# Beacon attention with a maxout FFN on one core: batch 0's waits, an order of scores, and the order of three loads

## The chip, the core and the metric

The kernel runs on one core of one Trainium2 chip. The core has a matrix engine (PE, whose weight loads are listed apart as PEld), a vector engine (DVE), a scalar engine (ACT), a general engine (POOL), and SP, which here only starts DMA transfers. Each engine takes its own instructions strictly in the order in which the program wrote them, and waits for others by semaphores. DMA transfers are started from SP's, ACT's and POOL's streams. The metric is the time of one execution on the device in microseconds (us); a kernel's time is the median of several.

## What is computed

```python
def _attn_ref(q, k, v, beacon_k, beacon_v):       # B=8, H=8, S=576, Nb=16, D=64
    k_all = np.concatenate([beacon_k, k], axis=2)
    v_all = np.concatenate([beacon_v, v], axis=2)
    scores = scale * np.matmul(q, k_all.transpose(0, 1, 3, 2))
    causal = np.zeros((S, Nb + S), dtype=bool)
    causal[:, Nb:] = np.triu(np.ones((S, S), dtype=bool), k=1)
    scores = np.where(causal, -1000000000.0, scores)
    a = np.exp(scores - scores.max(-1, keepdims=True))
    a /= a.sum(-1, keepdims=True) + 1e-09
    return np.matmul(a, v_all)

def _moe_ref(x, w1, w2, w3, w_out):               # 4608 tokens, 512 -> 768 -> 512
    h = np.maximum(np.maximum(x @ w1, x @ w2), x @ w3)
    return h @ w_out
```

The attention's output, with its heads side by side, is x. Inputs and output are float32; the kernel computes in bfloat16 with float32 sums.

## The kernel before

**Tiles.** Two heads make a pair `p` (four pairs in a batch), two pairs a quad (two quads in a batch), so batch 0 holds pairs 0 to 3 and quads 0 and 1, and quad 2 is the first of batch 1. Queries and keys of a pair are needed with the head dimension on the partitions, so PE transposes ("turns") them into PSUM, and DVE or ACT copies the result into `qkT`. The scores of a pair are made in four groups `(p, 0)` to `(p, 3)`: PE writes a group into one of two `sc` buffers (L464), ACT takes its exponential into `at_sb` (L473), and DVE (L490) or POOL (L492) zeroes what the causal mask removes. Then PE multiplies with the values and with ones (the row sums) for a quad and a half of its queries: `P(quad, half, apart, first, last)` is that step or some of its four passes (L536). ACT inverts the sums by Ln and Exp (`invert_sums`, L556 and L558), DVE multiplies (`multiply`, L568) into `xT`, the FFN's input. `F(n)` makes n units of the FFN; the first ones in batch 0 are half-units of eight 256-column matmuls (L615) into `fps`. The first three of these use weight 0, the next three weight 1.

**Order.** The order is written out by hand: `start()`, then the list `first_steps` for batch 0, whose entries each give a group of scores to be made and the functions to be called after it, then a planned loop for the other batches. In the list:

- `T(p, h, pv, q_copy, idle)` turns half h of pair p (`turn_half`, L393): six transposes of queries into one PSUM bank, six of keys into another, each followed by a copy into `qkT` (L413). `pv` says whether the banks are the two `pv` banks or two buffers of `fps`, which has two. `idle` transposes of a constant tile `busy` may be put ahead (`fill`, L387), into a part of the bank that nobody reads.
- `keep_busy(n, cols, ffn)` (L429) makes n matmuls of `busy`, 128 x `cols`, that nobody reads, into the bank `pv1` or a buffer of `fps`.
- `M(p, g, dve)` is the mask of a group, on DVE or POOL. `V(t)` is POOL's cast of a part of batch 0's values, `cast_p` POOL's cast of beacon keys.
- `load_w(i, 0, d_ff)` (L309) is two requests on POOL for weight i, with a cast to bfloat16 on the way.
- `G(0)` is `load_wide` (L182) for quad 2's queries, with a gate: DVE sets one column of the staging tile to zero (L187), and the request on SP waits for that. `load_wide(n_quad, 1)` is the same for the keys, with no gate. `CW(2, i)` is POOL's cast of these (L237), `turn_quad` and `TW` are PE's turns of them (L373) and their copies (L380).
- `next_load(n)` takes the next n loads from a list: SP's requests for quad 3 and batch 1's values, further on quad 4 and so on.

SP's stream holds only requests and their waits, so those of `next_load` follow the gated request of quad 2 as soon as they stand next, whatever the other engines do. A staging tile `st` is one of eight; the casts free it.

Of the kernel before, what the change touches and what calls it, by code (L numbers as in the profile page):

```python
# [16 lines left out]
def kernel(  # L17
# [19 lines left out]
    d_model, d_ff = moe_w1.shape  # L37
# [26 lines left out]
    n_quad = 2  # L64
# [99 lines left out]
    def pv_bank(i, shape, dtype):  # L164
        return pv_psum.tile(shape, dtype, name=f"pv{i}")
# [221 lines left out]
    def fill(ps, n):  # L387

        for i in range(n):
            x0 = 512 + 128 * (i % 4)  # L390
            nc.tensor.transpose(ps[:, x0 : x0 + 128], busy[:, 0:128], ident)

    def turn_half(p, h, pv, q_copy=None, idle=0):  # L393
        for i in range(2):
            src = stage.pop(("half16", p, h, i))
            if pv:
                bank = pv_bank(i, [128, 1024], BF16)
            else:
                bank = ffn_psum.tile([128, 1024], BF16, name="fps")
            ps = bank[:, 0:HALF]  # L400
            if i == 0:
                fill(bank, idle)
            for r in range(HR):
                for e in range(2):
                    nc.tensor.transpose(  # L405
                        ps[64 * e : 64 * e + 64, r * QP : (r + 1) * QP],
                        src[:, e, r],
                        ident[0:QP, 0:QP],
                        tile_position=(0, 64 * e),
                    )  # L410
            x0 = i * Nb + HALF * h
            dst = (qTs, kTs)[i][p % NT][:, x0 : x0 + HALF]
            (q_copy if i == 0 and q_copy else by_dve)(  # L413
                dst.rearrange("d (p r) -> d p r", r=HR), ps.rearrange("d (r p) -> d p r", r=HR)
            )
# [272 lines left out]
    def emit_ffn(limit, pool=None, name="fps"):  # L688
        if done[0] == len(units):
            return False  # L690
        need, fn, args = units[done[0]]
        if done[0] + 1 <= limit + 1e-6 and need <= ready[0]:
            fn(*args, pool or ffn_psum, name)
            done[0] += 1
            return True
        return False
# [8 lines left out]
    def L(fn, *a):  # L705
        return lambda: fn(*a)
# [28 lines left out]
    def start():  # L735
# [22 lines left out]
        cast_half(0, 1, by_act)  # L758
        by_dve(bk16_0, bk32_0)
        turn_half(0, 0, False, by_act)  # L760
        keep_busy(4)
        turn_beacons(0, 1, bk16_0)
        by_act(qk_all[:, 1:PPB, S : S + Nb], bT[:, 1:PPB, 0:Nb])
        cast_half(1, 0, by_dve)
        cast_half(1, 1, by_dve)
        keep_busy(2)
        turn_half(1, 0, True, by_act)

    pv_at = {}
# [4 lines left out]
    def steps(p):  # L774
        return [[0, 1], [2, 3]]

    def T(p, h, pv, q_copy=None, idle=0):
        def run():
            turn_half(p, h, pv, q_copy, idle)

        return run

    def M(p, gi, dve=False):
        return L(emit_masks, p, gi, dve)

    def P(quad, hf, apart=False, first=0, last=len(passes)):
        return L(emit_pv, quad, hf, first, last, apart)

    def V(t):
        return L(cast_first_v, t)  # L790

    def G(i):
        return L(load_wide, n_quad, i, nc.vector)

    def F(n):
        return lambda: [emit_ffn(END) for _ in range(n)]

    def CW(quad, i):
        return L(cast_wide, quad, i, by_pool)

    def TW(quad, i, n, act=False):
        return L(turn_wide, quad, i, n, by_act if act else by_dve, False)

    def cast_p():
        for g in range(n_quad):
# [6 lines left out]

    first_steps = [
        ((0, 0), [T(2, 0, False)]),
        ((1, 0), [T(3, 0, True, None, 4), L(next_load, 2), V(0)]),
        ((2, 0), []),
        ((3, 0), [T(0, 1, False, None, 4), M(0, 0, True), V(1), L(load_w, 0, 0, d_ff), V(2)]),
        ((0, 1), [T(1, 1, True), M(1, 0, True), M(0, 1)]),
        ((0, 2), [T(2, 1, False), M(2, 0, True), M(0, 2), V(3), V(4), L(load_w, 1, 0, d_ff)]),
        ((0, 3), [T(3, 1, False), M(3, 0, True), M(0, 3, True)]),  # L820
        ((1, 1), [M(1, 1)]),
        ((1, 2), [P(0, 0, False, 0, 2), M(1, 2)]),
        ((1, 3), [P(0, 0, False, 2, 4), invert_sums, M(1, 3, True)]),
        ((2, 1), [P(1, 0, True, 0, 2), multiply, M(2, 1), cast_p]),
        ((2, 2), [P(1, 0, True, 2, 4), invert_sums, M(2, 2, True), G(0), L(load_wide, n_quad, 1)]),
        ((2, 3), [P(0, 1, False, 0, 2), multiply, M(2, 3), CW(2, 0), L(load_w, 2, 0, d_ff)]),
        ((3, 1), [P(0, 1, False, 2, 4), invert_sums, F(1), M(3, 1, True)]),
        ((3, 2), [F(1), multiply, L(turn_beacons, 1, B_PE, bk16_1), L(next_load, 5), M(3, 2, True)]),
        ((3, 3), [F(1), M(3, 3, True), CW(2, 1), L(turn_quad, 2, 0), F(1), TW(2, 1, 0), P(1, 1), invert_sums, TW(2, 1, 1, True),
                  L(place_quad_beacons, 2, by_act), F(1), multiply]),  # L830
    ]
    at_step(4, 0, C(cast_wide, 3, 0, by_pool))
# [7 lines left out]
    for b in range(2, B):  # L840
        p = b * PPB
# [6 lines left out]
    for b in range(B_PE, B):  # L848
        p = b * PPB
# [117 lines left out]
```

The softmax here doesn't subtract the row's maximum and nothing guards it: scores larger than these inputs give would overflow.

## Time and profile before

| | |
|---|---|
| median of 4 runs | 300.56 us (298.3 to 300.96) |
| profiled execution | 300.96 us, its span 299.2 us |
| mean granted PE clock | 0.98 |
| HBM read, written | 35.13 MB, 14.22 MB |
| PE's share of the chain that ended last | 88% |

The span runs from the first to the last recorded instruction; the execution's own time is somewhat longer. In the chain that ended last one follows, from the last instruction back, what released each step. PE's instructions around the change, in order of time, are these (start us, us, engine, line, operation, tiles; in brackets the idle time before it and what ended it):

```profile
9.41 0.40 PE L464 MATMUL sc<-qkT 64*128 64x288 bf16 x6
10.27 0.40 PE L464 MATMUL sc<-qkT 64*128 64x288 bf16 x6 [0.47 <-DVE qkT L413]
10.60 0.40 PE L391 MATMUL fps<-ident,busy 128*128 128x128 bf16 x4
10.93 0.45 PE L405 MATMUL fps<-ident,quad 96*64 96x96 bf16 x12
11.80 0.63 PE L464 MATMUL sc<-qkT 64*128 64x288 bf16 x4 [0.43 <-DVE qkT L413]
12.36 0.45 PE L405 MATMUL pv<-ident,quad 96*64 96x96 bf16 x12
12.73 0.33 PE L464 MATMUL sc<-qkT 64*128 64x288 bf16 x4
13.00 0.32 PE L405 MATMUL fps<-ident,quad 96*64 96x96 bf16 x6
13.55 0.32 PE L405 MATMUL fps<-ident,quad 96*64 96x96 bf16 x6 [0.24 <-DMA quad<-in_k_dram]
13.80 0.30 PE L464 MATMUL sc<-qkT 64*128 64x288 bf16 x2
14.56 0.81 PE L405 MATMUL fps<-ident,quad 96*64 96x96 bf16 x12 [0.46 <-DVE qkT L413]
```

The first line is scores (2, 0), the second (3, 0); then come T(0, 1) with its four fillers, (0, 1), T(1, 1), (0, 2), T(2, 1) in two halves, (0, 3), and T(3, 1), which waits for DVE to copy T(2, 1) out of the two `fps` buffers. A few more rows that the prediction uses: ACT stands idle 1.15 us before the exponential of (1, 1) at 15.94, whose matmuls PE made from 15.30. POOL casts the last values of batch 0 at 17.83 for 1.17 us, requests weight 1 at 18.94, has masks at 20.02 for 1.05 us and `cast_p` at 21.02 for 0.74 us. DVE's mask of (1, 3) is at 18.62 for 0.64 us. Weight 1's two requests took 6.4 and 7.8 us to land.

### The profile page before, as it was taken

The numbers are of one execution on the slowest core, as the hardware profiler recorded it, in microseconds if no ns is written. First come the engines' busy times: TensorE is split into PE (matmuls) and PEld (weight loads), VectorE is DVE, ScalarE is ACT, GpSimd is POOL, SyncE is SP. The second block draws the span as 40 slices with busy tenths as digits, with TensorE's granted clock in tenths as the row PEclk, the third lists the DMA queues.
The fourth block names the chain that finished last, engine by engine and source line by source line (L and its number), as shares of the span: only waits on it lengthen the run. The fifth ranks groups of instructions, "written<-read, shape, count | busy, mean of one in ns | idle before, by whom it ended". The sixth has DMA issues, their size and how long they took to land.

```text
span 299.2 us, 8565 instructions
## 1 busy us (share of the span) xinstructions
PE 286.4 (96%) x3548; PEld 152.9 (51%) x3548; DVE 173.4 (58%) x341; ACT 147.1 (49%) x231; POOL 121.6 (41%) x241
## 2 busy tenths in 40 slices
PE   8798899999999999999999999999999999999992
PEld 4545676454545445444546777544454554444441
DVE  3765565546666665646664656466646665373571
ACT  3875488856665355545555555455546521302200
POOL 7361398455456454637363736373415100000000
PEclk9958999999999999999999999999999999999998
DMA  8999979989938999999979999899431003003003
GB/s 157 206 170 319 231 210 296 196 276 251 211 84 199 205 242 221 196 198 255 235 183 223 238 253 203 187 186 234 110 128 37 2 2 123 18 3 140 0 10 133
DMA packets 83590, 50.66 MB, mean 169 GB/s; under 512 B 64224, under 2 KB 75232, under 8 KB 83552
## 3 DMA queue, kind: packets, MB, share of 16 engines
q1 hardware_dynamic: 77904, 45.50, 65.7%
q0 software_dynamic: 4048, 4.03, 8.4%
q10 hardware_dynamic: 1600, 0.59, 0.9%
q8 instruction: 28, 0.46, 0.7%
q14 instruction: 10, 0.08, 0.1%
HBM read 35.13 MB, written 14.22 MB: 165 GB/s over the span
## 4 chain that ended last, share of the span: by engine, by line
PE 88%; DVE 4%; ACT 3%; POOL 1%; DMA 1%; issue 1%; DVEq 0%
PE fps L596 32%; PE pv L536 13%; PE sc L596 12%; PE fps L632 10%; PE sc L464 10%; PE sc L632 4%; PE fps L615 2%; PE pv L432 2%; ACT at_sb L473 1%; PE pv L373 1%; DMA out_dram<-y 1%; DVE xT L568 1%; DVE qkT L380 1%; POOL p L237 1%; PE fps L405 1%
## 5 line engine op out<-in xcount | busy, mean ns | idle before, releaser
L473 ACT ACTIVATE at_sb<-sc 128x928 bf16<-128x928 f32 (+5 forms) x128 | 103.8, 861 | 86.5 <-PE sc L464 84.6
L596 PE MATMUL fps<-xT,w_sb 128*128 128x512 bf16 (+1 forms) x488 | 110.2, 357 | 0.5 <-DVE xT L568 0.5
L492 POOL TENSOR_SCALAR_AFFINE_SELECT at_sb<-at_sb 128x256 bf16<-128x256 bf16 (+2 forms) x146 | 53.4, 386 | 103.8 <-ACT at_sb L473 102.8
L596 PEld LDWEIGHTS <-w_sb 128*128 128x128 bf16 x672 | 61.6, 98 | 65.0 <-issue 12.0
L606 DVE TENSOR_TENSOR hT<-hT,fps 128x512 bf16<-128x512 bf16 x72 | 49.4, 688 | 33.8 <-PE fps L596 33.8
L596 PE MATMUL sc<-xT,w_sb 128*128 128x512 bf16 (+1 forms) x184 | 42.1, 356 | 0.0
L464 PE MATMUL sc<-qkT 64*128 64x288 bf16 (+5 forms) x400 | 36.7, 284 | 2.3 <-DVE qkT L413 0.9
L632 PE MATMUL fps<-w_out_sb,hT 128*128 128x512 bf16 x150 | 36.0, 379 | 0.0
L640 DVE COPY y<-fps 128x512 f32<-128x512 f32 x25 | 17.3, 692 | 27.6 <-PE fps L632 26.3
L632 PEld LDWEIGHTS <-hT 128*128 128x128 bf16 x210 | 19.8, 98 | 24.0 <-DVE hT L606 1.9
L606 DVE TENSOR_TENSOR hT<-hT,sc 128x512 bf16<-128x512 bf16 x30 | 20.6, 688 | 16.4 <-PE sc L596 16.2
L536 PE MATMUL pv<-at_sb,v_sb 128*32 128x288 bf16 (+5 forms) x1376 | 29.7, 232 | 0.0
L604 DVE CAST hT<-fps 128x512 bf16<-128x512 f32 x31 | 21.4, 692 | 12.8 <-PE fps L596 12.8
L568 DVE TENSOR_TENSOR xT<-pv,recip 128x288 bf16<-128x288 f32 (+2 forms) x93 | 27.3, 348 | 2.3 <-ACT recip L558 2.2
L464 PEld LDWEIGHTS <-qkT 64*128 64x128 bf16 x400 | 14.5, 95 | 26.4 <-issue 18.9
L536 PEld LDWEIGHTS <-v_sb 128*32 128x32 bf16 (+1 forms) x1408 | 24.9, 98 | 3.3 <-issue 1.7
L248 POOL CAST p<-st 96x768 bf16<-96x768 f32 x32 | 25.6, 826 | 0.0
L287 POOL CAST v_sb<-st 128x1536 bf16<-128x1536 f32 (+2 forms) x21 | 18.4, 897 | 0.0
L536 PE MATMUL pv<-at_sb,ones 128*32 128x288 bf16 (+4 forms) x500 | 17.7, 263 | 0.0
L556 ACT ACTIVATE lnd<-pv 128x288 f32<-128x288 f32 x31 | 12.9, 416 | 8.0 <-PE pv L536 8.0
L237 POOL CAST p<-st 128x1152 bf16<-128x1152 f32 x12 | 13.7, 1145 | 5.5 <-DVE xT L568 5.5
L604 ACT CAST hT<-sc 128x512 bf16<-128x512 f32 x6 | 3.5, 586 | 23.7 <-PE sc L596 23.7
(73 smaller groups left out, 173.6 us busy)
## 6 DMA issues: line engine op xcount, KB each, us to landing
out_dram<-y SPq DMA_DIRECT2D x35, 256.0 KB, 2.4
st<-in_v_dram SPq DMA_DIRECT2D x23, 256.0 KB, 6.8
st<-in_q_dram SPq DMA_DIRECT2D x16, 288.0 KB, 4.3
st<-in_k_dram SPq DMA_DIRECT2D x16, 288.0 KB, 5.2
st<-in_q_dram SPq DMA_DIRECT2D x6, 576.0 KB, 6.5
st<-in_k_dram SPq DMA_DIRECT2D x6, 576.0 KB, 7.1
w_sb<-in_moe_w_dram POOLq DMA_DIRECT2D x6, 384.0 KB, 7.4
q_dram<-p SPq DMA_DIRECT2D x16, 144.0 KB, 2.3
```

Source lines behind the costliest of these rows:

```text
L248: cast(part.rearrange("p r h d -> p h r d"), st[0:QP, i * NQ2 : (i + 1) * NQ2].rearrange("p (h r d) -> p h r d", h=2, r=QR),)
L287: cast(v_sb[0:n, t:t1].rearrange("p t h d -> p (t h d)"), st[0:n, (t - t_lo) * H * D : (t1 - t_lo) * H * D],)
L464: nc.tensor.matmul(ps[:, e, off : off + q1 - q0], kT[hs, 128 * t : 128 * t + 128], qT[hs, q0:q1], start=True, stop=True, tile_position=(64 ...
L473: nc.scalar.activation(out=both_heads(p, gi), in_=ps[:, :, 0 : g_width(p, gi)], func=AF.Exp, scale=scale)
L492: nc.gpsimd.affine_select(out=view, in_=view, compare_op=ALU.is_ge, fill=0.0, base=x0, pattern=[[0, 2], [1, hi - lo]], channel_multiplier=-1,)
L536: nc.tensor.matmul(ps[bank][32 * j : 32 * j + 32, lo + q0 - qa : lo + qb - qa], lhsT, at_view(pair_of(quad, j)[0], t, pair_of(quad, j)[1], ...
L568: nc.vector.tensor_mul(xT[:, 2 * g + part - 1, c0 + ca : c0 + cb], ps[bank][:, lo : lo + cb - ca], recip[:, ca:cb],)
L596: nc.tensor.matmul(ps[:, o0 : o0 + n], w_in[i][:, ct, 128 * ft : 128 * (ft + 1)], xT[:, ct, x0 : x0 + n], start=(ct == 0), stop=(ct == n_c ...
L604: (by_act if alone[0] else by_dve)(h, ps)
L606: nc.vector.tensor_max(h, h, ps)
L632: nc.tensor.matmul(ps, hT[:, ft, 128 * tt : 128 * (tt + 1)], w_out_sb[:, ft, :], start=(ft == 0), stop=(ft == n_ft - 1),)
L640: nc.vector.tensor_copy(y, ps)
```

## The change

The numbers of `idle` become two, so that the key bank of a turn can have fillers too. `keep_busy` stands at three more places. Scores (1, 1) go ahead of T(3, 1), and T(3, 1)'s mask with it. `G(0)` and the key load go from step (2, 2) to step (1, 3). Weight 1 goes from step (0, 2) to (2, 1), behind `cast_p`; weight 2 from (2, 3) to (3, 3), behind `CW(2, 1)`. In the last step the fourth half-unit of the FFN goes behind the first turn of quad 2's keys.

```diff
-    def turn_half(p, h, pv, q_copy=None, idle=0):
+    def turn_half(p, h, pv, q_copy=None, idle=(0, 0)):
...
-            if i == 0:
-                fill(bank, idle)
+            fill(bank, idle[i])
...
-        ((1, 0), [T(3, 0, True, None, 4), L(next_load, 2), V(0)]),
-        ((2, 0), []),
-        ((3, 0), [T(0, 1, False, None, 4), M(0, 0, True), V(1), L(load_w, 0, 0, d_ff), V(2)]),
+        ((1, 0), [T(3, 0, True, None, (4, 0)), L(next_load, 2), V(0)]),
+        ((2, 0), [L(keep_busy, 2, 320, True)]),
+        ((3, 0), [T(0, 1, False, None, (4, 0)), M(0, 0, True), V(1), L(load_w, 0, 0, d_ff), V(2), L(keep_busy, 2)]),
         ((0, 1), [T(1, 1, True), M(1, 0, True), M(0, 1)]),
-        ((0, 2), [T(2, 1, False), M(2, 0, True), M(0, 2), V(3), V(4), L(load_w, 1, 0, d_ff)]),
-        ((0, 3), [T(3, 1, False), M(3, 0, True), M(0, 3, True)]),
-        ((1, 1), [M(1, 1)]),
+        ((0, 2), [T(2, 1, False, None, (0, 6)), M(2, 0, True), M(0, 2), V(3), V(4)]),
+        ((0, 3), [M(0, 3, True), L(keep_busy, 2)]),
+        ((1, 1), [T(3, 1, False), M(3, 0, True), M(1, 1)]),
         ((1, 2), [P(0, 0, False, 0, 2), M(1, 2)]),
-        ((1, 3), [P(0, 0, False, 2, 4), invert_sums, M(1, 3, True)]),
-        ((2, 1), [P(1, 0, True, 0, 2), multiply, M(2, 1), cast_p]),
-        ((2, 2), [P(1, 0, True, 2, 4), invert_sums, M(2, 2, True), G(0), L(load_wide, n_quad, 1)]),
-        ((2, 3), [P(0, 1, False, 0, 2), multiply, M(2, 3), CW(2, 0), L(load_w, 2, 0, d_ff)]),
+        ((1, 3), [P(0, 0, False, 2, 4), invert_sums, M(1, 3, True), G(0), L(load_wide, n_quad, 1)]),
+        ((2, 1), [P(1, 0, True, 0, 2), multiply, M(2, 1), cast_p, L(load_w, 1, 0, d_ff)]),
+        ((2, 2), [P(1, 0, True, 2, 4), invert_sums, M(2, 2, True)]),
+        ((2, 3), [P(0, 1, False, 0, 2), multiply, M(2, 3), CW(2, 0)]),
         ((3, 1), [P(0, 1, False, 2, 4), invert_sums, F(1), M(3, 1, True)]),
         ((3, 2), [F(1), multiply, L(turn_beacons, 1, B_PE, bk16_1), L(next_load, 5), M(3, 2, True)]),
-        ((3, 3), [F(1), M(3, 3, True), CW(2, 1), L(turn_quad, 2, 0), F(1), TW(2, 1, 0), P(1, 1), invert_sums, TW(2, 1, 1, True),
+        ((3, 3), [F(1), M(3, 3, True), CW(2, 1), L(load_w, 2, 0, d_ff), L(turn_quad, 2, 0), TW(2, 1, 0), F(1), P(1, 1), invert_sums, TW(2, 1, 1, True),
                   L(place_quad_beacons, 2, by_act), F(1), multiply]),
```

More of the change, by code (lines that the diff above doesn't have):

```diff
@@ L775, in steps, with T @@
         return [[0, 1], [2, 3]]
-    def T(p, h, pv, q_copy=None, idle=0):
+    def T(p, h, pv, q_copy=None, idle=(0, 0)):
         def run():
```

## The prediction

> **What bounds the kernel now.** First the head of the page: who is busy, and at which granted clock. (Tenths in 40 slices of 7.48 us.)
>
> ```profile
> span 299.2 us, 8565 instructions
> PE 286.4 (96%) x3548; PEld 152.9 (51%) x3548; DVE 173.4 (58%) x341; ACT 147.1 (49%) x231; POOL 121.6 (41%) x241
> PEclk9958999999999999999999999999999999999998
> ```
>
> PE bounds the whole, and the one place where its clock is low is slices 3 and 4, inside batch 0, which the change edits. From 36 us to the end PE's waits on other engines are single ones of 0.2 to 0.3 us, so what is won or lost before 36 us should reach the end. The busy times by stretch, with boundaries put where the clock turns:
>
> ```profile
> 10.65:14.06 3.41, 2.68 (x52) 1.59 (x51) 2.66 (x10) 2.81 (x4) 0.98 (x2) 1.00 1.38 236
> 14.06:17.47 3.41, 2.95 (x46) 1.58 (x45) 3.41 (x10) 2.26 (x4) 1.95 (x5) 0.50 1.16 176
> 17.47:20.89 3.42, 3.42 (x62) 1.45 (x62) 1.90 (x7) 2.42 (x6) 3.06 (x7) 0.50 0.85 155
> 20.89:24.30 3.41, 3.41 (x66) 1.94 (x62) 1.13 (x5) 2.06 (x4) 1.19 (x4) 0.50 1.03 189
> 27.72:31.13 3.41, 1.93 (x23) 1.54 (x22) 2.96 (x8) 1.02 (x3) 2.27 (x4) 1.00 1.06 388
> ```
>
> Columns: PE, PEld, DVE, ACT, POOL busy, clock, DMA share, GB/s. From 14.06 to 24.30 PE runs at half clock and is busy all the time from 14.56: PE is the bound there, while ACT is busy 2.26+2.42+2.06 = 6.74 of 10.24 us. Then the chain of waits, in order of time (start, us, what), up to the first pass of P(1,1):
>
> ```profile
> 13.47 0.66 DVE at_sb L490 x3
> 14.14 0.38 DVE qkT L413
> 14.56 0.81 PE fps L405 x12
> ...
> 28.86 1.14 POOL p L237
> 30.00 1.02 POOL w_sb L309 x2
> 31.02 1.16 POOL p L237
> 32.23 0.45 PE fps L373 x5
> 32.68 1.43 PE pv L536 x55
> ```
>
> PE stands at 28.6 until the first cast of quad 2, and at 31.6 until the second, which is behind weight 2's two requests on POOL. The table of waits gives both, and SP's own wait:
>
> ```profile
> PE pv L373 <- POOL p L237: 1.5, 1, 1.5
> PE fps L373 <- POOL p L237: 0.6, 1, 0.6
> SPq L189 <- DVE st L187: 8.8, 1, 8.8
> ```
>
> SP stood 8.8 us for the one-column memset of G(0), done at 21.95. The query for quad 2 left at 21.98 and took 6.8 us, so it landed at about 28.8, when the cast began; that the table of waits puts POOL's 5.5 us down to a multiply on DVE is only a coincidence of time.
>
> [...] 10.65 to 14.06 had PE busy 2.68 us, mostly transposes, and lost the clock; 27.72 to 31.13 had only 1.93, mostly 256-column matmuls, and kept it. [...] weight 2, requested among SP's loads, took 7.5 and 10.3 us to land (halves), weight 0 took 6.0 and 7.4.
>
> **The change part by part**, against the profiled execution: 300.96 us, of which 1.76 lie around the span. It stands 0.40 above the median of 300.56.
>
> *Fillers.* A transpose filler took 0.33/4 = 0.083 us (8.77 to 9.10 in the chain); 320-column ones 0.30 to 0.33 each at the start, at a clock that the record doesn't settle, so a pair costs 0.3 to 0.65. After (2,0): gap 0.47 before scores (3,0), which wait for DVE's copy. After T(0,1): gap 0.43 before (0,1), the same. Price there 0 to 0.4 in all; I take 0, DVE covers both. Six transposes ahead of the key turn of pair 2: 0.50 in a gap of 0.24 (the key quad's DMA), so that turn and (0,3) are 0.26 late; its copy on DVE is behind masks until 14.14, and ACT is in earlier exponentials until 14.2: nothing. The pair after (0,3): 0.3, or 0.5 at half clock, with nothing over it: the gap of 0.46 at 14.1 closes since scores (1,1) no longer stand behind T(3,1), which waited for DVE to empty the two buffers.
>
> *(1,1) ahead of T(3,1).* ACT idled 1.15 us until 15.94. (1,1) now follows (0,3) and the pair: ready at 15.0 at full clock, 15.5 at half; ACT gains 0.9 or 0.4. What is late next is T(3,1)'s copies, now behind M(0,3) on DVE; scores (3,1) use them 8 us later. Cost nothing. In half-clock time PE pays about 0.5 for the pair, as it is the bound then.
>
> *The clock.* If full clock holds, ACT bounds the stretch instead: at most its idle time, 10.24 − 6.74 = 3.5 us, is won; if the clock drops just as before, nothing. This is the unknown; a later drop is the first rival.
>
> *Quad 2's request.* G(0) and load_wide move behind mask (1,3), which ended at 19.26 (18.62 + 0.64): 2.6 us sooner at the old clock, about 17.7 (4.2 sooner) at full clock, where I count the exponentials on ACT from 15.0 back to back (0.98+0.78+0.65) plus the mask. With 6.8 to land: 26.1 or 24.5. Two casts of 1.14, no request between (−1.02): ready at 28.4 or 26.8 against 32.18. PE's waits of 1.5 and 0.6 go. SP issues quad 3's and batch 1's loads right behind this gate, so these all move forward too.
>
> *Weight 1* moves behind cast_p on POOL: 18.94 becomes 21.8 at the old clock, about 20.8 at full clock (value casts until 19.0, three masks 1.05, cast_p 0.74). Its second request goes 0.54 later and takes, by the halves seen, 7.8 to 10.3 us now that four wide loads lie ahead of it: lands at 29.2 to 31.7, or 30.1 to 32.6. I take the lower end, since the wide loads' big packets moved at 330 to 410 GB/s. First reader: the fourth half-unit (F), which stood at 30.57 and is now behind the turn of quad 2's keys. At full clock it is wanted at 27.3, so PE waits 1.9 for it; it ends at 30.2, and P(1,1), queued behind it, begins there instead of 32.61: gain 2.4. At the old clock PE comes out of the third F at 29.1 (28.6 + 0.5), turns both (1.0), finds weight 1 at 30.1, and starts P(1,1) at 31.1: gain 1.5.
>
> *Weight 2* moves behind both casts: requested at 27 to 29 instead of 29.94; its first reader comes after 47. Nothing. Batch 1's value cast stood at 42.54 and its first reader at 45.61; its loads move forward with the gate, so it follows.
>
> Sum: −1.5 to −2.4, taken −2.0: 300.96 − 2.0 = **299.0 us**.
>
> **Rivals.** (a) *The drop comes later and costs more.* At full clock PE is idle more than before: ACT bounds it, then weight 1 holds it for 1.9 us. If one window passes with much over the 1.48 us idle that 27.72 to 31.13 survived, the clock is halved at 27.7 or 31.1, over 256-column matmuls that fill PE. Three windows at half clock cost 10.24/2 = 5.1; less the 2.4: 300.96 + 2.7 = 303.7. One window only costs 1.7: 300.3. For it: the wait on weight 1. Against: real matmuls surround it. (b) *Clock held and weight 1 in time* (it lands by 27.3, 6 us, as weight 0's first half did): P(1,1) at 28.3, gain 4.3: 296.7. For it: DMA was at 106 to 114 GB/s at 19 to 21, room for the earlier loads. Against: 7.8 us for weight 1 in a quieter time. (c) *The change doesn't hold the clock:* the six fillers are transposes, and three pairs of matmuls may not be enough; the pair's 0.5 pushes P(0,1) later and the clock is regained where it was or one window later (1.7), and weight 1 comes at 31: gain 0 to 1, about 300.4. For it: three windows at 100% busy with short matmuls didn't restore the clock.
>
> **How the numbers follow.** Likeliest 0.40 at 299.0; (a) 0.15; (b) 0.20; (c) 0.25. About 1% (3.0 us) is what this measurement tells from no change. Faster by more than that, below 297.6: (b) and a part of the likeliest where weight 1 lands early, 0.25. Slower, above 303.6: the three-window end of (a) and a late weight 1, 0.11. The rest, 0.64. The range: 296.5 takes in (b) but not its best third (0.06), 302.0 takes in (c) and the one-window end of (a), and leaves out 0.12.
>
> **What would show it.** Clock: the 0.50 stretch from 14 to 24 gone or shorter. Fillers: the gaps of 0.47 and 0.43 filled and scores (3,0), (0,1) at the same times. (1,1): ACT's idle of 1.15 at 15.9 gone. Quad 2: SP's wait of 8.8 at least 2.6 shorter, POOL's casts back to back and done by 28.4. Weight 1: PE waiting on its DMA ahead of the fourth F. I am wrong if the clock is lost just as long at another place, or if PE waits on the casts as before.

## The result and the profile after

| | before | changed |
|---|---|---|
| median | 300.07 us (61 runs) | 301.80 us (40 runs) |
| ratio, 95% interval | | 1.0063 [1.0049, 1.0077] |
| profiled execution, its span | 300.96, 299.2 us | 301.24, 299.3 us |

The change makes the kernel slower by 0.6%, some 1.9 us. The forecast was 299.0, so the sign was wrong, though the time lies in the range. (The median of before is that of all its runs by then, 300.07 instead of 300.56.) A ratio, here and below, leaves out runs more than 1.5% above the fastest of their kernel.

The two spans differ by 0.1 us only, which hides the loss. PE's last rows, before and then changed (start us, us, engine, line, operation; each line number of the changed kernel is one lower):

```profile
293.22 0.66 PE L652 MATMUL sc<-w_out_sb,hT 128*128 128x192 bf16 x6
```

```profile
295.11 0.66 PE L651 MATMUL sc<-w_out_sb,hT 128*128 128x192 bf16 x6
```

PE ends 1.89 us later, as the ratio says. In this one execution of before, the last two output transfers took 3.6 and 3.8 us to land, in that of the changed kernel 1.8 and 2.0; the change touches neither. So I compare PE's dates, not spans.

The head of the changed kernel's page, with the chain's shares by engine:

```profile
PE 285.6 (95%) x3560; PEld 152.8 (51%) x3560; DVE 172.4 (58%) x341; ACT 147.1 (49%) x231; POOL 122.0 (41%) x241
PEclk9999799999999999999999999999999999999999
PE 83%; DMA 8%; DVE 3%; ACT 2%; POOL 2%; issue 1%; POOLq 0%; DVEq 0%
```

The low clock in slices 3 and 4 is gone, a shorter one is in slice 5, and DMA has 8% of the chain where it had 1%. The chain of waits of the changed kernel around that place:

```profile
20.72 0.50 POOL w_sb L309
21.22 10.90 DMA w_sb<-in_moe_w_dram
32.12 0.05 issue
32.16 1.43 PE fps L614 x6
33.60 2.44 PE pv L535 x48
```

Before, this stretch of the chain ran through POOL's casts. Now it is one transfer, the second half of weight 1, 10.9 us long. What PE does meanwhile, in order of time:

```profile
26.78 0.66 PE L373 MATMUL pv<-ident,p 128*128 128x128 bf16 x9
27.28 0.44 PE L373 MATMUL fps<-ident,p 128*128 128x128 bf16 x5
29.46 0.39 PE L614 MATMUL fps<-xT,w_sb 128*128 128x256 bf16 x2 [1.74 <-DMA w_sb<-in_moe_w_dram]
32.16 1.43 PE L614 MATMUL fps<-xT,w_sb 128*128 128x256 bf16 x6 [2.31 <-DMA w_sb<-in_moe_w_dram]
33.53 1.15 PE L535 MATMUL pv<-at_sb,ones 128*32 128x288 bf16 x20
34.47 1.74 PE L535 MATMUL pv<-at_sb,v_sb 128*32 128x288 bf16 x56
```

Quad 2's queries are turned at 26.78 (before: 30.06), its keys at 27.28 (32.23): 3.3 and 5.0 us sooner. Then the fourth half-unit of the FFN waits, 1.74 us for the first half of weight 1 and 2.31 for the second. P(1,1) begins at 33.53 (32.61), 0.9 us later, and it also runs slower, at a clock of 0.51 up to 35.68, instead of 1.00: in the two chains it ends at 36.0 instead of 34.1, another 1.0 us. Together that is the 1.9 us at PE's end. Busy times by stretch (PE, PEld, DVE, ACT, POOL, clock, DMA share, GB/s):

```profile
25.43:28.85 3.42, 2.19 (x28) 1.62 (x26) 3.42 (x9) 1.59 (x3) 2.17 (x3) 1.00 1.05 253
28.85:32.26 3.41, 0.49 (x3) 0.21 (x4) 0.40 (x1) 0.00 (x0) 0.00 (x0) 1.00 1.09 247
32.26:35.68 3.42, 3.42 (x54) 2.24 (x57) 0.69 (x1) 0.00 (x0) 0.00 (x0) 0.51 1.10 221
```

After 3.41 us with 0.49 us of PE work the clock is halved, just when PE gets its data. I call 3.41 us a window, for in the first 40 us of all the profiles half clock, where there is any, lasts 3.41 us or a whole multiple of it: 3.42 here, 3.4 in ten stretches of the experiments, 6.8 in e6, 10.24 in before (14.06 to 24.30), 10.2 in e3 and e4, 13.7 in e10 and 17.1 in e12. Where a profile has two stretches, they begin 13.7 (e5), 20.5 (e3, e10) or 23.9 us (e12) apart, which is four, six or seven windows. And last SP's and POOL's requests, in order of time:

```profile
18.18 0.38 SPq L189 DMA_DIRECT2D st<-in_q_dram  x1
18.61 0.47 SPq L189 DMA_DIRECT2D st<-in_k_dram  x1
19.12 0.80 SPq L189 DMA_DIRECT2D st<-in_q_dram  x1
19.97 0.91 SPq L189 DMA_DIRECT2D st<-in_k_dram  x1
20.67 1.08 POOL L309 DMA_DIRECT2D w_sb<-in_moe_w_dram  x2
20.92 1.02 SPq L267 DMA_DIRECT2D st<-in_v_dram  x1
```

Weight 1 (20.67) stands behind four wide loads, of quads 2 and 3, and the values of batch 1 come right behind it. Before, it was requested 3 us ahead of all of these, at 18.94. What the DMA queues moved shows the delay (packets, MB, share of the time of 16 engines; q1 is SP's queue, q0 POOL's), first from 21 to 24 us, then from 24 to 30:

```profile
q1 hardware_dynamic: 513, 1.12, 99.9%
```

```profile
q0 software_dynamic: 263, 0.75, 64.1%
q1 hardware_dynamic: 417, 0.89, 42.0%
```

In the first three microseconds POOL's queue has no row: nothing of weight 1 is moved while SP's wide loads are. And from weight 1's request to its landing POOL's queue moved 1.08 MB, where weight 1 is 0.79 MB in bfloat16. The rest, about 0.3 MB, must be of weight 2, which is now requested at 26.56 (before: 29.94), ahead of weight 1's landing. The prediction put that move at nothing; no run makes it alone, so its share in the loss stays open.

### The profile page after: what moved, and what is told of

Read it like the earlier page. It is cut to its first block, busy times and chain, and to the rows that moved or that the text cites. A ratio compares the mean times of both kernels' runs of the same rounds, so it can differ in the third digit from the quotient of the medians.

```text
span 299.3 us, 8591 instructions
## 1 busy us (share of the span) xinstructions
PE 285.6 (95%) x3560; PEld 152.8 (51%) x3560; DVE 172.4 (58%) x341; ACT 147.1 (49%) x231; POOL 122.0 (41%) x241
## 4 chain that ended last, share of the span: by engine, by line
PE 83%; DMA 8%; DVE 3%; ACT 2%; POOL 2%; issue 1%; POOLq 0%; DVEq 0%
PE fps L595 32%; PE sc L595 12%; PE pv L535 12%; PE fps L631 11%; PE sc L463 8%; PE sc L631 4%; DMA w_sb<-in_moe_w_dram 4%; DMA st<-in_v_dram 3%; DMA quad<-in_k_dram 2%; PE fps L614 2%; PE pv L373 1%; ACT at_sb L472 1%; DVE qkT L380 1%; DVE y L639 1%; DVE xT L567 1%
## 5 line engine op out<-in xcount | busy, mean ns | idle before, releaser
L463 PE MATMUL sc<-qkT 64*128 64x288 bf16 (+5 forms) x400 | 35.7, 277 | 1.6 <-DVE qkT L380 0.7
L535 PE MATMUL pv<-at_sb,v_sb 128*32 128x288 bf16 (+5 forms) x1376 | 29.5, 231 | 1.0 <-issue 1.0
L567 DVE TENSOR_TENSOR xT<-pv,recip 128x288 bf16<-128x288 f32 (+2 forms) x93 | 27.3, 349 | 2.7 <-ACT recip L557 2.7
L614 PE MATMUL fps<-xT,w_sb 128*128 128x256 bf16 x96 | 13.1, 282 | 4.0 <-DMA w_sb<-in_moe_w_dram 4.0
```

The source lines that it names most:

```text
L463: nc.tensor.matmul(ps[:, e, off : off + q1 - q0], kT[hs, 128 * t : 128 * t + 128], qT[hs, q0:q1], start=True, stop=True, tile_position=(64 ...
L535: nc.tensor.matmul(ps[bank][32 * j : 32 * j + 32, lo + q0 - qa : lo + qb - qa], lhsT, at_view(pair_of(quad, j)[0], t, pair_of(quad, j)[1], ...
L567: nc.vector.tensor_mul(xT[:, 2 * g + part - 1, c0 + ca : c0 + cb], ps[bank][:, lo : lo + cb - ca], recip[:, ca:cb],)
L614: nc.tensor.matmul(ps[:, f], w_in[i][:, ct, 128 * (ft + f) : 128 * (ft + f + 1)], xT[:, ct, tb * TOKB + lo : tb * TOKB + hi], start=(ct == 0),
```

## The experiments

I had three theories of the loss at first: (A) weight 1's later request alone; (B) the loads that SP pulls forward behind the earlier gate; (C) the fillers and the moved scores. When A failed in its size I formed (D): PE needs three things at the end of batch 0, quad 2's queries, quad 2's keys and weight 1; they share the engines with whatever else is requested, and the last of the three sets the end, in whichever order they are asked for. Its rival (E): weight 1 is slow just because it stands behind quad 2.

All results first. "Wait" is PE's wait for the three transfers or their casts in the one profiled execution, "P(1,1)" its beginning there.

| kernel | ratio to before, 95% interval | wait, us | P(1,1), us |
|---|---|---|---|
| before | 1 | 2.1 | 32.61 |
| changed | 1.0063 [1.0049, 1.0077] | 4.0 | 33.53 |
| e1_w1_back | 1.0007 [0.9984, 1.0031] | 4.3 | 33.99 |
| e2_fillers | 0.9982 [0.9960, 1.0004] | 4.7 | 34.14 |
| e3_loads | 1.0067 [1.0043, 1.0091] | 4.2 | 35.66 |
| e4_gate_only | 0.9990 [0.9969, 1.0011] | 0.8 | 31.97 |
| e5_hold3 | 0.9982 [0.9952, 1.0012] | 4.1 | 34.37 |
| e6_w1_back_hold3 | 1.0015 [0.9985, 1.0045] | 4.1 | 33.48 |
| e7_fill_wait | 0.9988 [0.9967, 1.0010] | 28 fillers | 33.56 |
| e8_w1_back_late | 0.9966 [0.9932, 1.0000] | 2.0 | 31.24 |
| e9_order | 0.9959 [0.9935, 0.9983] | 2.1 | 30.45 |
| e10_order_no_fill | 1.0011 [0.9982, 1.0040] | 2.3 | 35.04 |
| e11_hold3_late | 0.9972 [0.9951, 0.9992] | 2.5 | 30.56 |
| e12_transposes_only | one run, 304.79 us | 2.3 | 36.28 |
| e13_hold_fill | 0.9953 [0.9930, 0.9976] | 12 fillers | 32.45 |
| e14_order_fill | 0.9976 [0.9949, 1.0002] | 2.2 and 10 fillers | 31.10 |

A single profile is one draw: it differs from the median of its kernel by up to 2.7 us (e10's), and the windows and the transfers fall differently in each. Half clock began at 14.06 in before's, 13.7 in e3's, 13.8 in e4's and 11.0 in e10's, though PE's instructions are the same up to there. The verdicts rest on the ratios, the causes on what the profiles have in common.

**Which part of the change.** `e2_fillers` is before with the fillers and the moved scores alone, `e3_loads` before with the moved loads and the moved half-unit alone; together they make the change. The lines of e2, against before (and `turn_half` as in the change):

```diff
+        ((2, 0), [L(keep_busy, 2, 320, True)]),
+        ((3, 0), [..., V(2), L(keep_busy, 2)]),
+        ((0, 2), [T(2, 1, False, None, (0, 6)), ..., L(load_w, 1, 0, d_ff)]),
+        ((0, 3), [M(0, 3, True), L(keep_busy, 2)]),
+        ((1, 1), [T(3, 1, False), M(3, 0, True), M(1, 1)]),
```

And those of e3:

```diff
+        ((0, 2), [T(2, 1, False), M(2, 0, True), M(0, 2), V(3), V(4)]),
+        ((1, 3), [..., G(0), L(load_wide, n_quad, 1)]),
+        ((2, 1), [..., cast_p, L(load_w, 1, 0, d_ff)]),
+        ((2, 2), [P(1, 0, True, 2, 4), invert_sums, M(2, 2, True)]),
+        ((2, 3), [P(0, 1, False, 0, 2), multiply, M(2, 3), CW(2, 0)]),
+        ((3, 3), [..., CW(2, 1), L(load_w, 2, 0, d_ff), L(turn_quad, 2, 0), TW(2, 1, 0), F(1), P(1, 1), ...
```

> The kernel before with the fillers and the moved scores alone; all loads as before. Theories A and B: the clock holds from 14 us on, PE reaches the turn of quad 2 earlier and waits longer for its casts there, but since the gate on DVE comes earlier too, P(1,1) begins at about 31 instead of 32.6: ratio 0.993 to 0.997. Theory C: the fillers don't pay or the clock is lost later, ratio 1.000 or more.

> The kernel before with the three moved loads and the moved half-unit alone; no fillers, scores in the old order. Theories A and B: half clock from 14 to 24 as before, the casts are done before PE is ready for them, and weight 1, requested at about 21.8, lands at about 32.5: PE waits 2 to 3 us for it and P(1,1) begins at 33.5 or later: ratio 1.003 to 1.010. Theory C: the loads are the gain, ratio 0.993 to 0.998.

The loads alone cost what the whole change costs: 1.0067. Their trace has half clock from 13.7 to 24 as before, quad 2 done when PE comes, and then:

```profile
PE fps L615 <- DMA w_sb<-in_moe_w_dram: 4.2, 2, 2.4
```

So theory C is out: the fillers are not the loss. Nor do they win what A and B expected of them: 0.9982, its interval reaching 1. In that trace PE comes to quad 2 at 26.2, 2.3 us sooner than before, and waits there:

```profile
PE pv L373 <- POOL p L237: 4.7, 1, 4.7
```

Its time at full clock was turned into a longer wait, and in that wait, at 30.5, the clock was halved for 3.4 us.

**Weight 1 back.**

```diff
-        ((0, 2), [T(2, 1, False, None, (0, 6)), M(2, 0, True), M(0, 2), V(3), V(4)]),
+        ((0, 2), [T(2, 1, False, None, (0, 6)), M(2, 0, True), M(0, 2), V(3), V(4), L(load_w, 1, 0, d_ff)]),
...
-        ((2, 1), [P(1, 0, True, 0, 2), multiply, M(2, 1), cast_p, L(load_w, 1, 0, d_ff)]),
+        ((2, 1), [P(1, 0, True, 0, 2), multiply, M(2, 1), cast_p]),
```

> The changed kernel with weight 1's two requests back in step (0, 2), ahead of POOL's masks and cast_p. Theory A (the later request of weight 1 is the loss, the rest of the change gains): weight 1 is requested at about 18.6 instead of 20.7 and lands by 27, PE's waits of 4.0 us on it go, the clock is not lost at 32, P(1,1) begins at about 28.5 instead of 33.5, and the time is about 297 us, ratio to before 0.985 to 0.993. Theory B (the loads that SP pulls forward are the loss, wherever weight 1 stands on POOL): weight 1 still takes about 10 us, lands at 28.5 to 29.5, and PE waits 1.5 to 2.5 us: ratio 0.992 to 0.998. Theory C (the fillers and the moved scores are the loss): ratio 1.000 or more.

The ratio, 1.0007, fits neither A nor B; it is in C's range, but e2 and e3 have ruled C out. Against the changed kernel the step wins 0.6% by the ratios, 0.3% by the medians (301.10 against 300.31 of before in the same session), so weight 1's request is a good part of the loss. But the wait didn't go; it changed its name:

```profile
PE pv L373 <- POOL p L237: 2.8, 1, 2.8
PE fps L373 <- POOL p L237: 1.5, 1, 1.5
```

Weight 1 is in time, and quad 2's queries, requested at 18.73, are cast only at 28.31, its keys at 30.44 (24.06 and 25.46 in the changed kernel). This gave theory D.

**The gate alone.** Before, with only `G(0)` and the key load moved.

```diff
-        ((1, 3), [P(0, 0, False, 2, 4), invert_sums, M(1, 3, True)]),
+        ((1, 3), [P(0, 0, False, 2, 4), invert_sums, M(1, 3, True), G(0), L(load_wide, n_quad, 1)]),
...
-        ((2, 2), [P(1, 0, True, 2, 4), invert_sums, M(2, 2, True), G(0), L(load_wide, n_quad, 1)]),
+        ((2, 2), [P(1, 0, True, 2, 4), invert_sums, M(2, 2, True)]),
```

> The kernel before with quad 2's two loads moved to step (1, 3) alone; weight 1 and weight 2 requested where they were, no fillers. Theory A: weight 1, requested at 18.9, lands by 28 and PE, at half clock until 24, wants it at about 30: no wait; quad 2's casts come about 2 us sooner and PE's waits of 1.5 and 0.6 us mostly go: ratio 0.993 to 0.997. Theory B: weight 1 takes 10 us and more, lands at 29 to 30, and the gain is small: ratio 0.997 to 1.002.

0.9990: nothing that can be told from 1. That is B's range, though not B's reason, since PE does not wait for weight 1 here. In its profile the casts come 1.1 us sooner, P(1,1) 0.6; requested 2.5 us sooner, quad 2 took 8.3 us to its cast instead of 6.9.

**The crowd.** In these the loads of quad 3, and with them batch 1's values behind them on SP, wait for a gate of their own. All four have the first two lines of this diff, e5 and e6 the rest too; e6 and e8 also have weight 1 as in e1:

```diff
-    loads += load_qk(1)[2:] + load_v_pieces(1)
+    loads += [L(load_wide, 3, 0, nc.vector), L(load_wide, 3, 1)] + load_v_pieces(1)
...
-        ((2, 3), [..., M(2, 3), CW(2, 0)]),
+        ((2, 3), [..., M(2, 3), L(next_load, 2), CW(2, 0)]),
...
-        ((3, 2), [..., L(next_load, 5), M(3, 2, True)]),
+        ((3, 2), [..., L(next_load, 3), M(3, 2, True)]),
```

In `e5_hold3` and `e6_w1_back_hold3` it stands in step (2, 3), so the request goes at about 22; in `e8_w1_back_late` and `e11_hold3_late` in step (3, 2), at about 26.3. Weight 1 is at its new place in e5 and e11, at its old one in e6 and e8.

> The changed kernel with quad 3's two loads, and batch 1's value loads behind them on SP, held by a gate on DVE in step (2, 3), at about 22 instead of 19.1. Theory D (the wait at the end of batch 0 is one for bytes: quad 2, weight 1 and whatever was requested among them share the engines): quad 2 lands by 24.5 and weight 1 by 27 to 29 instead of 32.1; PE's wait on weight 1 falls from 4.0 to about 1, the clock is kept, P(1,1) begins at 28.5 to 30: ratio to before 0.990 to 0.997, unless PE then waits for batch 1's values. Theory E (weight 1 is slow by itself when it is requested behind the two loads of quad 2, whatever follows): it lands at 31 or later, ratio 1.003 to 1.007.

> The same gate for quad 3, with weight 1 back in step (0, 2). Theory D: the three transfers that PE needs, 1.9 MB, go first; quad 2's queries and keys land at about 25 and 26.5 instead of 28.3 and 30.4, weight 1 at about 27; P(1,1) begins at 28.5 to 29.5, no drop of the clock: ratio 0.988 to 0.996, unless the values of batch 1 become late. Theory E: quad 2 still lands at 28 or later beside weight 1, ratio 0.998 to 1.003.

> Weight 1 back in step (0, 2), and quad 3's and batch 1's value loads held until step (3, 2), about 27. Theory D: no crowd at all beside quad 2 and weight 1; quad 2 lands by 25, weight 1 by 26, P(1,1) begins at 28 to 28.5. But the values of batch 1, which took from 24 to 42 before, then land at 43 to 45, when PE wants them at about 41: it waits 2 to 4 us there, or its casts of quad 3 are late: ratio 0.995 to 1.005. If the values are not bound by the transfers, ratio 0.985 to 0.990.

> The changed kernel, weight 1 behind cast_p, with quad 3's and batch 1's value loads held until step (3, 2), about 27. Theory D: nothing is behind quad 2 on SP while weight 1 is moved, so quad 2 lands by 24 and weight 1, requested at 20.7, by 27.5 to 28.5; PE waits about 1 us; ratio 0.992 to 0.998. Theory E (slow behind the two loads of quad 2 alone): weight 1 at 30 or later, ratio 1.000 to 1.005.

The short hold gives no clear answer. e5, at 0.9982, is 0.8% below the changed kernel, just above D's range and against E, and cannot be told from e11. Its one profile, an execution of 302.5 us where the median is 300.15, has weight 1 landing at 33.1, so it does not show how the other runs gained. e6, at 1.0015, is in E's range and above D's: in its profile quad 2's keys, requested at 18.90, are cast only at 29.93. The long hold (e8, e11) shortens the wait. e11's PE in order of time:

```profile
26.51 0.44 PE L373 MATMUL fps<-ident,p 128*128 128x128 bf16 x5
27.93 0.39 PE L614 MATMUL fps<-xT,w_sb 128*128 128x256 bf16 x2 [0.97 <-DMA w_sb<-in_moe_w_dram]
29.80 0.83 PE L614 MATMUL fps<-xT,w_sb 128*128 128x256 bf16 x6 [1.48 <-DMA w_sb<-in_moe_w_dram]
30.56 0.68 PE L535 MATMUL pv<-at_sb,ones 128*32 128x288 bf16 x20
```

Weight 1, requested at 20.84, lands at 29.8 instead of 32.1, between D's 28.5 at most and E's 30 or later, and the kernel goes from 1.0063 to 0.9972. That is D's size of ratio and against E, whose 1.000 is above the interval. Both have a part: in this profile too POOL's queue moves hardly anything at first (one packet from 21.1 to 21.7, none from 21.3 to 21.8), while quad 2 is moved on SP's at 98 to 101% of the 16 engines' time; then weight 1's halves land at 27.9 and 29.8, where they landed at 29.5 and 32.1 in the changed kernel. So weight 1 waits behind quad 2 with the crowd or without, and the hold speeds up what comes after. And the values of batch 1 aren't missed, although the first of them is requested at 27 instead of 24 (e8's expectation feared 2 to 4 us): no pass of PE waits for them in e8 or e11, only POOL's cast waits 0.8 us in e11. With weight 1 back as well (e8) the interval is [0.9932, 1.0000], no different from e11; there weight 1 is moved first, and quad 2's keys are cast only at 27.7, where D had quad 2 landed by 25. Whether it is quad 3's 1.2 MB or the values' short packets behind them (from 30 to 32.2 in the changed kernel SP's queue moved 0.19 MB in 348 packets, from 21 to 24 1.12 MB in 513) that weigh on weight 1, these runs don't separate; both were held.

**The clock.** `e7_fill_wait` is the changed kernel with 28 more `busy` matmuls in the wait for weight 1; nothing else.

```diff
-... TW(2, 1, 0), F(1), P(1, 1), ...
+... TW(2, 1, 0), L(keep_busy, 28, 320, True), F(1), P(1, 1), ...
```

> The changed kernel with 28 more 320-column fillers (0.135 us each at full clock, 3.8 us) between the turn of quad 2's keys and the fourth half-unit, in the wait for weight 1. If the lost window of the clock costs what its arithmetic says (3.4 us at half clock over work that fills PE: 1.7 us), P(1,1) still begins at about 33 but the scores (4, 0) come at about 36 instead of 37.7, and the ratio to before is 1.000 to 1.002. If the wait on weight 1 alone is the cost and the clock is hidden, 1.005 to 1.007.

Its PE, at full clock throughout:

```profile
28.79 3.96 PE L431 MATMUL fps<-busy 128*128 128x320 bf16 x28 [0.24 <-DVE hT L622]
32.59 1.04 PE L614 MATMUL fps<-xT,w_sb 128*128 128x256 bf16 x8
33.56 0.68 PE L535 MATMUL pv<-at_sb,ones 128*32 128x288 bf16 x20
34.06 1.18 PE L535 MATMUL pv<-at_sb,v_sb 128*32 128x288 bf16 x56
```

P(1,1) begins at 33.56, where it began in the changed kernel (33.53), and the scores (4, 0) come at 36.71 instead of 37.69. Weight 1 is as late as it was, and the kernel goes to 0.9988. So the lost clock is a cost of its own, about 0.75% or 2.2 us between the two ratios, 1.0 us in the two profiles. But e7's ratio leaves out five of its 21 runs; over all of them its mean is 301.3 against 300.4 of before, 1.003, which is half of the changed kernel's loss. The granted clock of all runs fits a cost of more than one window: one window at half clock is 3.41 × 0.5 / 299 = 0.0057 of the mean. By that I count windows, which is an estimate: half clock behind PE's last row is in the mean too, 1.9 us in before's profile, or 0.003. Of the changed kernel's 41 executions none has a mean clock of 1; ten have 0.992 to 0.994 (one window lost), 28 have 0.987 to 0.989 (two), three less. Before has 0.983 or 0.977 in most: three or four windows. The fillers and moved scores do save one or two windows of three or four. What e7 pays is seen too: in six of its 21 runs the mean clock is 0.987 to 0.994 and the time 302.7 to 306.5, 3 to 7 us above the others. The lost windows alone cost at most (1 − 0.987) × 299 = 3.9 us. None of these six has a trace, so it stays open what else is in them.

`e12_transposes_only` is the changed kernel without its three pairs of matmul fillers.

```diff
-        ((2, 0), [L(keep_busy, 2, 320, True)]),
+        ((2, 0), []),
-        ((3, 0), [..., V(2), L(keep_busy, 2)]),
+        ((3, 0), [..., V(2)]),
-        ((0, 3), [M(0, 3, True), L(keep_busy, 2)]),
+        ((0, 3), [M(0, 3, True)]),
```

> The changed kernel without its three pairs of matmul fillers; the six transposes and the moved scores stay. If only matmuls hold the clock, it falls to half at about 14 as before, PE comes to the turn of quad 2 at 28.5 or later, and weight 1 is late all the same. If the transposes and the shorter gaps suffice, the clock is full to 30.

In this one run the clock was half from about 10.9 to 28.0, five windows, so the six transposes and the moved scores did not hold it. With one run, and before itself at three or four windows, that is a sign and no proof that the three pairs do.

**Versions that beat both.** `e9_order` has the fillers, quad 2's early request, weight 1 at its old place, the long hold, and the fourth half-unit ahead of the turn of quad 2's keys as before, so that PE has work between two landings. `e10_order_no_fill` has these loads without the added fillers. `e13_hold_fill` is e11 with 12 fillers in what is left of the wait, `e14_order_fill` e9 with 10. Step (3, 3) in the changed kernel, e9, e13 and e14 (the hold and weight 1 as in the diffs above):

```diff
-... L(turn_quad, 2, 0), TW(2, 1, 0), F(1), P(1, 1), ...
+... L(turn_quad, 2, 0), F(1), TW(2, 1, 0), P(1, 1), ...
+... L(turn_quad, 2, 0), TW(2, 1, 0), L(keep_busy, 12, 320, True), F(1), P(1, 1), ...
+... L(turn_quad, 2, 0), L(keep_busy, 10, 320, True), F(1), TW(2, 1, 0), P(1, 1), ...
```

e10 is before with the gate of e4, the long hold, and weight 2 behind `CW(2, 1)`.

> Fillers and moved scores as changed; quad 2's request early; weight 1 back in step (0, 2); quad 3's and batch 1's value loads held until step (3, 2), about 27; and the fourth half-unit back ahead of the turn of quad 2's keys, so that it runs while PE would wait for these keys. Theory D (bytes): weight 1 lands at about 27, quad 2's keys at 27.6, PE is fed between them, the clock is kept, P(1,1) begins at 29.4 and scores (4, 0) come at 32.7: ratio to before 0.988 to 0.993. If batch 1's values, or quad 3's casts, are late instead, PE waits for them between 36 and 45: 0.994 to 1.000.

> The same loads without any of the added fillers and with the scores in the old order: half clock from 14 to 24. If the transfers alone set the end of batch 0 (theory D taken to its end), PE comes to the turn of quad 2 at 28.7 to 29 and finds everything there, P(1,1) begins at 30.6 to 31.2, and the fillers are worth only 1.2 to 1.8 us: ratio 0.993 to 0.997. If holding the clock is worth its full 3.5 us once nothing is late, 1.000 or more here beside 0.988 for the kernel with fillers.

> The changed kernel with quad 3's and batch 1's value loads held until step (3, 2), and 12 more 320-column fillers (1.6 us) in what is left of the wait for weight 1. If the crowd behind quad 2 and the lost clock are the two costs and they add, the clock is full in nearly all runs (it was in 8 of 20 without these fillers), P(1,1) begins at 30 to 30.6 and the ratio to before is 0.991 to 0.995. If the lost clock no longer matters once weight 1 lands by 29.8, it stays at 0.996 to 0.999.

> The kernel with weight 1 back in step (0, 2), the same hold, and the fourth half-unit ahead of the turn of quad 2's keys, with 10 more 320-column fillers (1.4 us) ahead of that half-unit. Where clock and crowd add: full clock in nearly all runs, P(1,1) at 30.3, ratio 0.991 to 0.995. If not, as without these fillers, 0.994 to 0.998.

e9, 0.9959, and e13, 0.9953, are faster than before by 0.2 to 0.7%; less than expected, since e9's wait is still 2.1 us and its clock fell in 15 of its 22 runs (a mean of 0.994 or less). e13's ratio leaves out four of its 17 runs; its median over all, 298.69 against 300.11, agrees with the ratio, but its mean, 299.96 against 300.28, gives 0.999. e9's PE:

```profile
28.41 0.83 PE L614 MATMUL fps<-xT,w_sb 128*128 128x256 bf16 x6 [1.43 <-DMA w_sb<-in_moe_w_dram]
29.91 0.61 PE L373 MATMUL fps<-ident,p 128*128 128x128 bf16 x5 [0.67 <-POOL p L237]
30.45 1.15 PE L535 MATMUL pv<-at_sb,ones 128*32 128x288 bf16 x20
```

Without the fillers (e10) the same loads give 1.0011: PE came at 29.5 and waited 2.3 us more for the queries, cast at 30.6 though requested at 20.3. So the fillers with the moved scores are worth about 0.5% when the transfers are in order; intervals of 0.3% each leave that rough, and it is far from the 1.2% that the expectation has for a full gain. That crowd and clock add up is not shown: e13's point is below e11's, but their intervals overlap and the means over all runs do not agree with it, and e14 is not better than e9. Three of the four runs of e13 above 303 us are again longer than their lost windows alone make them.

## Why the prediction was wrong

- **Fillers free, scores (1, 1) earlier, clock held from 14 to 24:** right. Scores (3, 0) begin at 10.34 (10.27 before) and (0, 1) at 11.87 (11.80), ACT's idle of 1.15 us at 15.9 is gone, the clock is 1.00 there. The key turn of pair 2 waits 0.33 for its DMA, not for the fillers.
- **Quad 2's request and casts:** right to some tenths. SP's request at 18.18 (said: 17.7, though the terms given there, 15.0 + 0.98 + 0.78 + 0.65 + 0.64, make 18.1), landing after 5.8 us (6.8), both casts done at 26.6 (26.8), PE ready for the fourth half-unit at 27.7 (27.3).
- **Weight 1's landing: here it failed.** The request was as said (20.67; 20.8). "I take the lower end, since the wide loads' big packets moved at 330 to 410 GB/s": the second half took 10.9 us, not 7.8, and landed at 32.1, beyond even the upper end of 31.7. The rate of the wide loads was not the error. The page counts bytes written: weight 1's 2 × 384 KB are bfloat16, while 512 × 768 × 4 = 1.57 MB are read. (That it counts so can be worked out: float32 inputs of q, k, v (28.3), beacon keys and values (0.5) and four weights (6.3) make 35.1 MB, its "HBM read".) So the fall from 377 GB/s (21 to 25 us) to 251 (25 to 32) need not be one of speed. With POOL's 1.01 MB taken twice, the 1.75 MB of the second stretch are 2.76 MB read in 7 us, an estimate of 394 GB/s. What was too low is the amount of work ahead of weight 1 and beside it. SP's wide loads, for which I had widened the range to 10.3 us, had 99.9% of the engines' time from 21 to 24, and POOL's queue moved nothing then; batch 1's values, of which I wrote only that they "move forward too", and a part of weight 2 then shared the engines with it. The lower end, 7.8 us, was what a half of weight 1 took with none of this ahead of it.
- **The wait for it:** 4.0 us instead of 1.9, from the same term.
- **The clock in that wait:** rival (a) had the drop behind an idle wait, nearly its place (at 27.7 or 31.1; it was 32.3) and the price of a window ("One window only costs 1.7"), and e7 shows that it costs. It stood beside the sum, with 0.15, and with a wait of 1.9 us its one-window case was still a gain. But the two came together: the window with 0.49 us of PE work lies in the longer wait for weight 1. The prediction's P(1,1) at 30.2 stood for a gain of 2.4; it began 3.3 us later (33.53), and the clock made it about 1.0 us longer in this execution. −2.4 + 3.3 + 1.0 = +1.9, as measured.
- **The point behind it:** I added a gain at PE to a gain at the loads, as if each would reach P(1,1). e2 (PE's part alone) and e4 (the gate alone) each gain nothing that the measurement tells from 1. P(1,1) begins when the last of three transfers is there; PE coming sooner only waited longer (4.7 us in e2, 2.1 before).

## What to carry to other kernels

This stretch ended on loads. Moving one load ahead of another moved the wait to the other (4.0 us for weight 1 in the changed kernel, 4.3 us for quad 2's casts in e1), and what SP issues behind quad 2's moved request (21.98 to 18.18) moved along, batch 1's first values from 23.98 to 20.92: list all that will be in flight, in bytes read, and ask which lands last. Speeding the engine up to such a point gained nothing by itself that can be told from 1 (0.9982, e2) and lengthened its idle time (from 2.1 to 4.7 us), and the clock was half for 3.4 us from 30.5 on. Here asking earlier for what is needed won nothing that can be told from 1 (0.9990, e4); holding back what nobody needs yet turned the changed kernel's 1.0063 into 0.9972 (e11).

## What the runs showed of the hardware beyond that

- Half clock outlasted the idleness by far. In before, PE was idle for 0.73 of the 3.41 us up to 14.06, less than the 1.48 of 27.72 to 31.13 after which the clock stayed full, and for 0.46 more until 14.56. It was busy without a break from there, for two whole windows and most of a third, and the clock came back only at 24.30 (the prediction's "three windows at 100% busy" were 2.95 of 3.41 us and two full ones). After the wait that ended at 32.16 it took one window (to 35.68) in this execution; most runs of the changed kernel, 28 of 41, lost two in all by their mean clock.
- PE stood still in the middle of P(0,1), ahead of the same instruction, for 1.03 us in the changed kernel, 2.15 in e7 and 1.74 in e13, with nothing in the profile that released it. The changed kernel's row:

```profile
22.85 0.30 PE L535 MATMUL pv<-at_sb,v_sb 128*32 128x96 bf16 x9 [1.03 <-issue]
```

One 16 KB packet of the queue named "instruction" was moved between 20 and 22 us in each of the three. Whether that packet has to do with the gap is not shown: e8 has one between 18 and 22.5 too, and no gap; e11 and e1, with one there as well, have gaps of 0.4 and 0.35. In before, at half clock, there is none.
